# Splitting the transposes around block work, an earlier transpose of first rows, a later reciprocal

## Chip, cores and metric

The kernel runs on one core of a Trainium2 chip. The time is device time in microseconds; the figure compared is the median of several runs. A core has TensorE (PE; its weight loads are listed apart as PEld), VectorE (DVE), ScalarE (ACT), GpSimd (POOL) and SyncE (SP), which run side by side and wait for each other by semaphores.

## What is computed

Top-k attention, then a mixture of experts with one expert per token, all in fp32:

```python
# q, k, v: (B=8, H=8, S=576, D=64)
scores = matmul(q, k.T) / sqrt(D)
kth = partition(scores, -32)[..., -32]            # the 32nd largest of each row
scores = where(scores >= kth, scores, -1e9)
attn = exp(scores - max); attn /= sum(attn) + 1e-9
x = matmul(attn, v)                               # rearranged to (4608 tokens, 512)
logits = x @ w_gate                               # 8 experts
e = argmax(logits); gate = softmax(logits)[e]
y = gate * (relu(x @ w1[e]) @ w2[e])              # w1[e]: 512x1024, w2[e]: 1024x512
```

## The kernel before

The program is a list of 144 *turns*. Each takes two 128-row tiles of scores (128x576 each) through a pipeline that spreads over several turns:

- TensorE multiplies q and k into PSUM (`sc`), three turns ahead; ScalarE copies the result to SBUF (`s`).
- VectorE finds each row's 32nd largest score (`search`: folds into `h`, `l`, `few`, `hl`, then rounds of MAX8 and MATCH_REPLACE8 on `scr`, into `tops`).
- ScalarE (`low`, then `depths`), GpSimd (`less`) and ScalarE again (`weights`, the exponential) make the masked weights `w`.
- One turn later TensorE transposes `w` (`wTm`: 4 transposes for each of the two tiles; `wTl`: the last columns of both) and ScalarE copies the result to `wT` and `wTt`.
- Nine turns make two *units* of two heads. When a unit's tiles are through, `ending` multiplies by v (`po`, twice), turns the result back (`px`) and scales it with the reciprocals `rz` of the rows' sums.
- After 18 turns a batch is complete: its tokens are routed, and rows of one expert form *blocks* of 128 rows. TensorE does the blocks' work in *pieces*, 16 to a block, between the attention's instructions: the rows' transposes (`xtp`, copied to `xTs`), 8 pieces of `ph` (first product), 8 of `py` (second product).

TensorE's, ScalarE's and VectorE's instructions stand in the program as this loop issues them; nothing reorders them later.

```python
def bank(name):                               # two PSUM banks in turn, for all of
    return k.ps_t.tile([P, SM], F32, name=name, tag="t")   # wTm, wTl, po, px, rank

def transposed(tiles, w):
    q = slice(ST + tiles[0][1] * P, ST + (tiles[0][1] + 1) * P)
    for m, (n, i) in enumerate(tiles):
        pm = bank("wTm")
        for c in range(NC):                   # NC = 4
            ...
            nc.tensor.transpose(pm[:, c * P:(c + 1) * P], w[:, m, first:first + P], ident)
        ...                                   # ScalarE empties the bank into wT
    yield
    pt = bank("wTl")
    ...                                       # transposes of the last columns
    yield
    ...                                       # ScalarE copies them to wTt

def block(n, following=..., put_off=...):
    if not hasattr(n, "xT"):
        turned(n)                             # xtp, and the copy to xTs put on `due`
        yield "pause"
    evacuate("xT")
    ...                                       # 8 pieces of ph, 4 products each
    evacuate("h0")
    following()
    yield "pause"
    evacuate()
    ...                                       # 8 pieces of py

def following():
    put_stores()
    if loaded and landed(loaded[0]):
        turned(loaded[0])                     # the next block's rows

def pieces(n):
    nonlocal current, left
    while n > 0 and left > 0:
        if current is None:
            if not landed(loaded[0]):
                break
            current = block(loaded.pop(0), following, stores.append)
            ahead()
        if clock is None:
            evacuate()
        step = next(current)
        if step == "pause":
            if clock is not None:
                break
            continue
        ...

def ending(b, u):                             # yields the place in a turn where it goes on
    ...
    out_steps = outputs(n, x)
    yield "products"
    next(out_steps)                           # po, first half
    yield "relu"
    next(out_steps)                           # ScalarE copies it to oT
    if u % 2 == 0:
        yield "relu"
    div = divisors(n)
    next(div)                                 # ScalarE writes rz
    aside.append(div)                         # VectorE's reciprocal, in the next search
    yield "products"
    next(out_steps)                           # po, second half
    ...
    yield "relu"
    next(out_steps)
    yield "products"
    next(out_steps)                           # px
    yield "relu"
    next(out_steps, None)                     # ScalarE copies it to xl
    yield "rows"
    ...

# the loop over turns, from the scores' copies on
    evacuate()
    at_place("turn")
    turns = turning(i - 1) if i else iter(())
    next(turns, None)                         # wTm, both tiles
    part = min(BETWEEN, now - now // 2)       # BETWEEN = 2
    rest = pieces(part)
    next(turns, None)                         # wTl
    rest = pieces(now - now // 2 - part + rest)
    weights(tiles, w_of[i], nbias)
    next(turns, None)                         # copy to wTt
    evacuate()
    if i + AHEAD + 1 < len(work):
        multiply(i + AHEAD + 1)               # sc
    ...
    at_place("products")                      # po or px, if an ending is at that place
    at_place("weights")
    credit = min(credit + pieces(now // 2 + rest), 6 * rate)
```

Of the kernel before, what the change touches and what calls it, by code (L numbers as in the profile page):

```python
# [35 lines left out]
def kernel(  # L36
# [249 lines left out]
    def fold(s):  # L286

        f = SimpleNamespace()
        f.h = k.att.tile([P, 2, HF], F32, name="h", bufs=1)
        nc.vector.tensor_tensor(f.h, s[:, :, 0, :], s[:, :, 1, :], op=ALU.max)  # L290
        f.l = k.att.tile([P, 2, HF], F32, name="l")
        nc.vector.tensor_tensor(f.l, s[:, :, 0, :], s[:, :, 1, :], op=ALU.min)
        return f
# [8 lines left out]
    aside = []  # L302
# [85 lines left out]
                w[:, m, :], w[:, m, :], AF.Exp, scale=scale, bias=nbias[:, m:m + 1], accum_out=n.z[:, c:c + 1]  # L388
            )

    def transposed(tiles, w):

        q = slice(ST + tiles[0][1] * P, ST + (tiles[0][1] + 1) * P)
        for m, (n, i) in enumerate(tiles):
            pm = bank("wTm")
            for c in range(NC):
                first = c * P + (0 if tails(tiles) else m * ST)
                nc.tensor.transpose(pm[:, c * P:(c + 1) * P], w[:, m, first:first + P], ident)  # L398
            pm4 = pm[:, :].rearrange("p (c q) -> p c q", c=NC)
            if tails(tiles):  # L400
                at = tail_at(n)
                nc.scalar.copy(wT[:, :, :, at:at + ST], pm4.rearrange("p c (h q) -> p c h q", h=2))
            else:
                nc.scalar.copy(wT[:, :, m, q], pm4)  # L404
        yield
        pt = bank("wTl")
        if tails(tiles):
            for a in range(2):
                nc.tensor.transpose(pt[0:ST, a * P:(a + 1) * P], w[:, 1 - a, SM:S], ident)
        else:  # L410
            nc.tensor.transpose(pt[:, 0:P], w[:, :, :].rearrange("p m k -> p (m k)")[:, SM:SM + P], ident)
        yield
        if tails(tiles):
            pt4 = pt[0:ST, 0:2 * P].rearrange("p (a h q) -> p a h q", a=2, h=2)
            for h in range(2):
                both = wTt[h * ST:(h + 1) * ST, :].rearrange("p (a q) -> p a q", q=ST)[:, 0:NT + 1:NT, :]
                nc.scalar.copy(both, pt4[:, :, h, :])
        else:
            nc.scalar.copy(wTt[:, q], pt[:, 0:P])  # L419
# [248 lines left out]
    def evacuate(upto=None):  # L668

        while due and (upto is None or upto in [kind for kind, _ in due]):  # L670
            due.pop(0)[1]()
# [62 lines left out]
    with fast:  # L734
# [9 lines left out]
        waiting, loaded, coming, spare, scatters, stores = [], [], [], [], [], []  # L744
        current = None
        left = clock = 0

        def landed(n):
            return clock is None or clock - n.at >= ON_CHIP
# [16 lines left out]

        def following():
            put_stores()
            if loaded and landed(loaded[0]):
                turned(loaded[0])  # L770

        def pieces(n):
            nonlocal current, left
            while n > 0 and left > 0:
                if current is None:
                    if not landed(loaded[0]):
                        break
                    current = block(loaded.pop(0), following, stores.append)
                    ahead()
# [7 lines that stand above are left out]
                if step == "last":  # L787
                    current = None
                n -= 1
                left -= 1  # L790
            return n
# [11 lines left out]
        def ending(b, u):  # L803

            nonlocal left
            n = unit[b * U + u]
            if u == 0:
                x_of[b] = k.xp.tile([P, KC, XW], F32, name="x")
                in_turn(token_ids(x_of[b][:, :, Dm + 1].bitcast(I32), b))
                lg_of[b] = k.small.tile([P, KC, E], F32, name="lg")  # L810
            x, lg = x_of[b], lg_of[b]
# [6 lines that stand above are left out]
                yield "relu"  # L818
            div = divisors(n)
            next(div)  # L820
            aside.append(div)
            yield "products"
            next(out_steps)
            if b * U + u + 2 < len(units):
                load_values(unit[b * U + u + 2])
            yield "relu"
            next(out_steps)
            yield "products"
            next(out_steps)
            yield "relu"  # L830
            next(out_steps, None)
            yield "rows"
            through(div)
            logits(n, lg)
            rows(n, x)
            if u < U - 1:
                return
            yield "small"
            r = choice(lg)
            aside.append(r.steps)  # L840
            yield "weights"
            yield "turn"
            through(r.steps)
            nc.scalar.activation(lg, lg, AF.Exp)
            yield "products"
            ranks(r)
            yield "small"
            steps = places(r, x)
            aside.append(steps)
            yield "relu"  # L850
            nc.scalar.copy(run, r.run)
            yield "pool"
            through(steps)
            scatters.extend(scattering(r, x))
            if b == B - 1:
                scatter(KC)
                slot_i = k.small.tile([1, 2, NSLOT], I32, name="slot_i")
                through(table(slot_i, SURE, False))
                firsts = [(slot_i[0:1, 0, j:j + 1], slot_i[0:1, 1, j:j + 1]) for j in range(SURE)]
                ready = load_rows(SimpleNamespace(), firsts[0][1], True)  # L860
            new = LAST - SURE if b == B - 1 else new_of[b]
            if new:
                slot_i = slot_last if b == B - 1 else k.small.tile([1, 2, NSLOT], I32, name="slot_i")
                steps = table(slot_i, new, b == B - 1)
                aside.append(steps)
                yield "weights"
                yield "pool"
                yield "weights"
                yield "pool"
                through(steps)  # L870
                coming.extend((slot_i[0:1, 0, j:j + 1], slot_i[0:1, 1, j:j + 1]) for j in range(new))
            if b == B - 1:
                spare.extend(coming[ALWAYS - SURE:])
                del coming[ALWAYS - SURE:]
                assert len(loaded) == 2 and not waiting
                fill_up()
                coming[0:0] = [(firsts[0][0], ready)] + [(expert, (piece,)) for expert, piece in firsts[1:]]
                scatter(0)
# [3 lines left out]
        def at_place(name):  # L882
            for end in list(late):
                if end[1] == name:
                    end[1] = next(end[0], None)
                    if end[1] is None:
                        late.remove(end)
# [3 lines left out]
        def tiles_of(i):  # L891
            b, g = work[i]
            return [(unit[b * U + u], tile) for u, tile in g]

        def turning(i):
            return transposed(tiles_of(i), w_of.pop(i))

        def multiply(i):
            tiles = tiles_of(i)
            got_of[i] = products(tiles)  # L900
            n, tile = tiles[0]
            more = n.b * U + n.u + 2
            if tile == (NC - 1 if n.u % 2 else 2 * NC) and more < len(units):
                unit.append(load_unit(*units[more]))

        def loop():
            nonlocal credit, rate, clock
            for i in range(min(AHEAD, len(work))):
                multiply(i)
                s_of[i], steps = scores(got_of.pop(i))  # L910
                for step in steps:
                    step()
            multiply(AHEAD)
            f_of[0] = fold(s_of[0])
            fold_on(f_of[0])
            for i, (b, g) in enumerate(work):
# [36 lines left out]
                        step()  # L953
                evacuate()
                at_place("turn")
                turns = turning(i - 1) if i else iter(())
                next(turns, None)
                part = min(BETWEEN, now - now // 2)
                rest = pieces(part)
# [1 line left out]
                rest = pieces(now - now // 2 - part + rest)  # L961
                weights(tiles, w_of[i], nbias)
                next(turns, None)
                evacuate()
                if i + AHEAD + 1 < len(work):
                    multiply(i + AHEAD + 1)
                if tile == NC - 1:
                    end = ending(b, u)
                    late.append([end, next(end)])
                at_place("products")  # L970
                at_place("weights")
                credit = min(credit + pieces(now // 2 + rest), 6 * rate)
# [147 lines left out]
```

## Time and profile before

The time before is 1374.14 us, the median of three runs from 1371.75 to 1375.33; the profiled run's span is 1370.3 us.

| engine | busy us | share of the span | instructions |
|---|---|---|---|
| PE | 1234.6 | 90% | 7666 |
| PEld | 838.6 | 61% | 7666 |
| DVE | 1084.5 | 79% | 4591 |
| ACT | 932.0 | 68% | 2113 |
| POOL | 661.5 | 48% | 805 |

The groups that the change touches (mean time of one record; a matmul in fp32 leaves two records or more):

| group | count | busy us | mean ns |
|---|---|---|---|
| PE transposes `wTm` | 1152 | 171.2 | 289 |
| ACT copy `wT` from `wTm`, 128x512 | 256 | 139.1 | 604 |
| PE `ph`, 128x128 | 2560 | 308.6 | 276 |
| PE `py`, 128x512 | 640 | 292.2 | 596 |
| ACT copy `xTs` from `xtp`, 128x512 | 40 | 24.3 | 608 |
| DVE reciprocal `rz`, 128x10 | 32 | 6.4 | 200 |

A line of a wait names the engine that was idle, what it was to do next, and after `<-` what it waited for, with the time. "L398" is line 398 of the kernel. In the timeline a row merges instructions of one kind that follow each other: start, length, engine, line, what is written from what, shapes, how many records, and in brackets the idle time before it.

### The profile page before, as it was taken

What the parts mean: (1) busy time and instruction counts of PE and PEld (TensorE: products, weight loads), DVE (VectorE), ACT (ScalarE), POOL (GpSimd) and SP (SyncE); (2) the same over time, 40 slices, a digit from 0 to 9 for tenths busy, and PEclk for the clock granted to TensorE, in tenths of its full rate; (3) what the DMA queues carried; (4) which work ended last, traced back from release to release, by engine and by line L of the source; (5) the groups of instructions that cost most, each with busy time, mean ns of one, the idle gap of its engine ahead of it and who ended that gap; (6) DMA issues with size and microseconds to landing.
All of it is one profiled execution on the core that took longest, in us unless ns stands there. A gap on an engine that the chain in (4) does not pass through costs nothing. (4 is left out here: it accounts for less than half of the span.)

```text
span 1370.3 us, 24487 instructions
## 1 busy us (share of the span) xinstructions
PE 1234.6 (90%) x7666; PEld 838.6 (61%) x7666; DVE 1084.5 (79%) x4591; ACT 932.0 (68%) x2113; POOL 661.5 (48%) x805
## 2 busy tenths in 40 slices
PE   5777677687799999999999999999999999999995
PEld 3444444344466666766666666767676677776773
DVE  8999999999999999999999999999999820000000
ACT  4788877877888888888877788887777821111110
POOL 3455557555654666566556665565557621000000
PEclk8788787877999999999999999999999999999998
DMA  2100011001583267427654474357542859999880
GB/s 82 29 29 29 28 36 56 29 29 44 178 296 124 89 232 266 142 72 261 226 174 168 166 274 148 113 188 293 184 167 75 308 183 358 390 325 331 301 321 18
DMA packets 102220, 231.68 MB, mean 169 GB/s; under 512 B 5182, under 2 KB 25918, under 8 KB 102080
## 3 DMA queue, kind: packets, MB, share of 16 engines
q1 hardware_dynamic: 95328, 209.76, 43.8%
q0 software_dynamic: 6464, 19.97, 4.0%
q8 instruction: 62, 1.02, 0.3%
q14 instruction: 78, 0.64, 0.1%
q10 hardware_dynamic: 288, 0.30, 0.1%
HBM read 208.72 MB, written 22.33 MB: 169 GB/s over the span
## 5 line engine op out<-in xcount | busy, mean ns | idle before, releaser
L379 POOL TENSOR_TENSOR w<-s,w 128x576 f32<-128x576 f32 x288 | 409.5, 1442 | 432.3 <-ACT w L370 432.3
L687 PE MATMUL ph<-xTs,w 128*128 128x128 f32 x2560 | 308.6, 276 | 6.0 <-ACT xTs L664 6.0
L687 PEld LDWEIGHTS ph<-xTs,w 128*128 128x128 f32 x2560 | 297.4, 192 | 26.4 <-issue 19.1
L702 PE MATMUL py<-w,hT 128*128 128x512 f32 x640 | 292.2, 596 | 0.0
L338 DVE MAX8 tops<-scr 128x8 f32<-128x168 f32 x864 | 245.5, 316 | 0.0
L276 PE MATMUL sc<-qkb 64*128 64x288 f32 (+1 forms) x1280 | 221.6, 472 | 9.5 <-ACT s L283 5.2
L387 ACT ACTIVATE w<-w,nbias 128x576 f32<-128x576 f32 x288 | 224.0, 792 | 3.5 <-POOL w L379 2.5
L370 ACT ACTIVATE w<-s,low 128x576 f32<-128x576 f32 x288 | 207.6, 768 | 4.7
L398 PE MATMUL wTm<-turn,w 128*128 128x128 f32 x1152 | 171.2, 289 | 29.0 <-ACT xl L450 17.7
L398 PEld LDWEIGHTS wTm<-turn,w 128*128 128x128 f32 x1152 | 133.1, 146 | 89.6 <-issue 35.4
L999 DVE CAST any_i<-pd 1x1 int32<-1x1 f32 x1 | 0.1, 146 | 236.0 <-PE pd L997 236.0
L702 PEld LDWEIGHTS py<-w,hT 128*128 128x128 f32 x640 | 114.4, 190 | 117.6 <-issue 116.5
L345 DVE MATCH_REPLACE8 scr<-tops,scr 128x168 f32<-128x168 f32 x576 | 176.9, 311 | 0.0
L283 ACT COPY s<-sc 128x576 f32<-128x576 f32 x288 | 169.1, 641 | 10.5 <-PE sc L276 10.5
L404 ACT COPY wT<-wTm 128x512 f32<-128x512 f32 x256 | 139.1, 604 | 38.9 <-PE wTm L398 38.6
L276 PEld LDWEIGHTS sc<-qkb 64*128 64x128 f32 (+1 forms) x1280 | 118.2, 195 | 72.9 <-issue 26.6
L432 PE MATMUL po<-wT,vb 128*64 128x288 f32 x1024 | 157.8, 457 | 0.4 <-ACT wTt L419 0.4
L708 POOL DMA_INDIRECT out_dram<-y,xg x40 | 43.1, 1078 | 211.9 <-ACT y L716 199.8
L329 DVE MAX8 few<-l 128x8 f32<-128x288 f32 x288 | 127.2, 442 | 0.0
L432 PEld LDWEIGHTS po<-wT,vb 128*64 128x64 f32 x1024 | 75.3, 152 | 78.0 <-issue 29.3
L692 ACT ACTIVATE hT<-ph 128x512 f32<-128x512 f32 x80 | 48.6, 608 | 107.3 <-PE ph L687 107.3
L290 DVE TENSOR_TENSOR h<-s 128x576 f32<-128x576 f32 x144 | 117.0, 812 | 5.8 <-ACT s L283 5.8
(116 smaller groups left out, 1433.4 us busy)
## 6 DMA issues: line engine op xcount, KB each, us to landing
w<-in_moe_w_dram SPq DMA_DIRECT2D x80, 2048.0 KB, 9.6
qkb<-in_qk_dram SPq DMA_DIRECT2D x31, 608.0 KB, 4.3
xg<-x_rows SPq DMA_DIRECT2D x40, 257.0 KB, 10.0
vb<-in_v_dram SPq DMA_DIRECT2D x32, 320.0 KB, 3.2
x_rows<-blank SPq DMA_DIRECT2D x5, 257.0 KB, 14.7
x_rows<-blank POOLq DMA_DIRECT2D x4, 257.0 KB, 8.5
x_rows<-x,posi POOLq DMA_INDIRECT x40, 3.1
out_dram<-y,xg POOLq DMA_INDIRECT x40, 6.1
```

The costliest lines, as they stand in the source:

```text
L276: nc.tensor.matmul(ps[rows, j, 0:HF], n.q[d, cols], n.k[d, keys], start=True, stop=True)
L283: lambda m=m, ps=ps: nc.scalar.copy(s[:, m, :, :], ps[:, :, 0:HF]) for m, ps in enumerate(got)
L338: nc.vector.max(out=tops[:, m, r * 8:(r + 1) * 8], in_=src[m])
L345: nc.vector.match_replace(out=scr[:, m, :], in_to_replace=tops[:, m, r * 8:(r + 1) * 8], in_values=src[m], imm_value=NEG,)
L370: nc.scalar.activation(w[:, m, :], s[:, m, :, :].rearrange("p j k -> p (j k)"), AF.Relu, scale=-STEEP, bias=low[:, m:m + 1],)
L379: k.last_pool = in_turn(nc.gpsimd.tensor_tensor(w[:, m, :], s[:, m, :, :].rearrange("p j k -> p (j k)"), w[:, m, :], op=ALU.subtract)).ins
L387: nc.scalar.activation(w[:, m, :], w[:, m, :], AF.Exp, scale=scale, bias=nbias[:, m:m + 1], accum_out=n.z[:, c:c + 1])
L398: nc.tensor.transpose(pm[:, c * P:(c + 1) * P], w[:, m, first:first + P], ident)
L404: nc.scalar.copy(wT[:, :, m, q], pm4)
L432: nc.tensor.matmul(po[r, 0:HF], n.v[:, c, r], rhs, start=(c == 0), stop=(c == KC - 1))
L687: nc.tensor.matmul(ph[:, f, :], n.w1[:, 0, dt, fc * P:(fc + 1) * P], n.xT[:, dt, :], start=(dt == 0), stop=(dt == DT - 1),)
L702: nc.tensor.matmul(py, hT[:, f, :], n.w2[:, 0, f, :], start=(f == 0), stop=(f == FT - 1))
```

## The change

Three things are done, and no arithmetic is added or removed.

- **Split transposes.** `wTm`, `wTl`, `po`, `px` and `rank` share two PSUM banks in turn. When an ending has put an output into one of them at the end of a turn, the next turn's second `wTm` needs that bank, and ScalarE has to empty it first. After such a turn (`busy_bank`) the second tile's transposes are now issued behind the first two pieces of block work.
- **First blocks' rows ahead.** A block whose predecessor has been finished before its weights had come gets its rows transposed by `block` itself, right ahead of its first product. Now the loop does it ahead of the scores, and `pieces` starts no block whose rows are not transposed.
- **Reciprocal later.** `divisors` joins the queue of side work for VectorE one step of the ending later.

```diff
-    def transposed(tiles, w):
+    def transposed(tiles, w, apart=False):
@@
                 nc.scalar.copy(wT[:, :, m, q], pm4)
-        yield
+            if m == 0 and apart:
+                yield
+        if not apart:
+            yield
         pt = bank("wTl")
@@ def following():
             put_stores()
-            if loaded and landed(loaded[0]):
+            if loaded and landed(loaded[0]) and not hasattr(loaded[0], "xT"):
                 turned(loaded[0])
@@ def pieces(n):
                 if current is None:
-                    if not landed(loaded[0]):
+                    if clock is not None and not hasattr(loaded[0], "xT"):
                         break
                     current = block(loaded.pop(0), following, stores.append)
@@ def ending(b, u):
             div = divisors(n)
             next(div)
-            aside.append(div)
             yield "products"
             next(out_steps)
             if b * U + u + 2 < len(units):
                 load_values(unit[b * U + u + 2])
             yield "relu"
             next(out_steps)
+            aside.append(div)
             yield "products"
@@ the loop
-                turns = turning(i - 1) if i else iter(())
+                turns = turning(i - 1, busy_bank) if i else iter(())
+                busy_bank = False
                 next(turns, None)
                 part = min(BETWEEN, now - now // 2)
                 rest = pieces(part)
@@
                 weights(tiles, w_of[i], nbias)
                 next(turns, None)
+                if current is None:
+                    following()
                 evacuate()
@@
                 if tile == NC - 1:
                     end = ending(b, u)
                     late.append([end, next(end)])
+                busy_bank = any(end[1] == "products" for end in late)
                 at_place("products")
```

(Cut: `turning` passes the flag on, and `busy_bank` starts as False.)

More of the change, by code (lines that the diff above doesn't have):

```diff
@@ L893, in tiles_of, with turning @@
             return [(unit[b * U + u], tile) for u, tile in g]
-        def turning(i):
-            return transposed(tiles_of(i), w_of.pop(i))
+        def turning(i, apart=False):
+            return transposed(tiles_of(i), w_of.pop(i), apart)
         def multiply(i):
@@ L955, in loop @@
                 at_place("turn")
-                turns = turning(i - 1) if i else iter(())
+                turns = turning(i - 1, busy_bank) if i else iter(())
+                busy_bank = False
                 next(turns, None)
```

## The prediction

> **What bounds the kernel now.** I read the page's busy table and its 40 slices first, then the stretches cut where the slices change, then the waits of the middle stretch alone, then the timeline around single waits.
>
> The four stretches (columns: us, then busy time and instruction count of PE, PEld, DVE, ACT and POOL, the granted clock, DMA share, GB/s):
>
> ```profile
> 0.00:350.00 350.00, 253.22 (x1358) 150.64 (x1360) 343.39 (x1482) 270.53 (x624) 182.47 (x246) 0.81 0.12 39
> 350.00:400.00 50.00, 42.53 (x280) 28.89 (x278) 50.00 (x211) 42.72 (x98) 30.45 (x38) 0.97 0.76 273
> 400.00:1090.00 690.00, 675.61 (x4508) 468.72 (x4505) 680.82 (x2847) 568.29 (x1300) 416.14 (x481) 1.00 0.52 184
> 1090.00:1345.00 255.00, 253.24 (x1482) 184.54 (x1481) 9.98 (x51) 48.96 (x93) 31.50 (x40) 1.00 0.85 302
> ```
>
> To 400 us VectorE (the top-32 search) is busy all the time but for the start, and TensorE has time to spare. From 400 to 1090 both are full: TensorE is idle 690 - 675.6 = 14.4 us, VectorE 690 - 680.8 = 9.2 us. From 1090 only expert blocks are left and TensorE alone sets the pace: the scalings of y come every 14.45 us (1326.5, 1340.9). So whatever this change does before 400 us is hidden behind VectorE, the last stretch holds the same blocks in both kernels, and the gain has to come out of the 14.4 us of TensorE and the 9.2 us of VectorE in the middle.
>
> Who waited for whom from 400 to 1090 us (total us, times, longest):
>
> ```profile
> ACT wT L404 <- PE wTm L398: 32.8, 22, 2.0
> ACT oT L434 <- PE po L432: 22.0, 28, 1.6
> ACT wT L402 <- PE wTm L398: 17.9, 9, 4.6
> ...
> PE ph L687 <- ACT xTs L664: 5.3, 5, 1.1
> DVE rz L457 <- ACT rz L455: 4.9, 6, 1.6
> PE wTl L411 <- ACT wT L404: 4.6, 16, 0.5
> DVE h L290 <- ACT s L283: 4.0, 4, 1.1
> ...
> PE wTm L398 <- ACT oT L434: 3.2, 3, 1.1
> ```
>
> With one more line of 1.3 us (the transposes waiting for the copy of xl) TensorE's waits add to 5.3 + 4.6 + 3.2 + 1.3 = 14.4 us, all its idle time. VectorE's two add to 8.9 of its 9.2 us. Two of the waits, on TensorE's timeline:
>
> ```profile
> 476.90 0.66 PE L398 MATMUL wTm<-turn,w 128*128 128x128 f32 x4 [1.11 <-ACT oT L434]
> 477.40 1.06 PE L687 MATMUL ph<-xTs,w 128*128 128x128 f32 x8
> 478.77 0.33 PE L411 MATMUL wTl<-turn,w 128*128 128x128 f32 x1 [0.31 <-ACT wT L404]
> ```
>
> ```profile
> 507.43 1.02 PE L702 MATMUL py<-w,hT 128*128 128x512 f32 x2
> 508.29 0.60 PE L662 MATMUL xtp<-turn,xg 128*128 128x128 f32 x4
> 508.73 0.27 PE L411 MATMUL wTl<-turn,w 128*128 128x128 f32 x1
> 510.06 1.16 PE L687 MATMUL ph<-xTs,w 128*128 128x128 f32 x8 [1.06 <-ACT xTs L664]
> ```
>
> In the first, the second tile's transposes want the bank that still holds an output, and ready block work (ph) stands behind them. In the second, a batch's first block has its rows transposed and its first product wants ScalarE's copy of them at once.
>
> **What the skill says.** The Trainium skill, "PSUM — Partial Sum Buffer", section "Engine vs sequencer instructions", says that TensorE may load weights ahead of matmuls in flight, but that matmuls start and complete in program order. The first timeline agrees: the ready ph products do not pass the waiting transposes (1.11 us). So moving instructions in the program can fill such a wait. The same sentence calls ScalarE's queue strictly first in, first out; that is the danger here, because a copy that must wait for later transposes holds up all of ScalarE. "Perfetto Trace Analysis", "Optimization Strategy", advises to look for gaps on the bounding engine within each regime; the split at 400 us is that. "SBUF — State Buffer", "Who interferes with whom", says that a VectorE instruction with two inputs in SBUF contends with a reading GpSimd instruction. The trace fits: the fold into h, two SBUF inputs, took 0.74 us at 644.29 and 1.68 us at 659.58, where GpSimd's small operations were long too. It adds noise whenever the phase of the engines shifts.
>
> **The change, part by part.** The built programs show what moves. On each engine the number of compute instructions stays. No piece of block work changes its turn except around six first blocks, and the last stretch is untouched.
>
> 1. *Split transposes.* 67 of the 144 turns get "4 transposes, up to two pieces, 4 transposes" for "8 transposes, pieces". None lies before turn 53, which waits near 410 us: earlier there are no pieces. Following TensorE's gaps from turn to turn over 400 to 1090 us, those that lie in a turn that is now split are: 3.2 us (transposes behind oT), 1.3 us (behind xl), and of the 4.6 us of wTl behind the first copy of wT 3.15 us, because two pieces and four transposes now come between. Each such wait, 0.3 to 1.3 us, is shorter than two pieces (1.06 us for ph here, 1.02 us for py, one piece each, so about 2 us). Sum 7.7 us.
> 2. *First blocks' rows ahead.* xtp and its copy move behind the wTl transposes and before the next scores; the first ph follows the scores (8 matmul records 1.24 us at 647.27) instead of standing right behind. The copy of xTs takes 0.63 us, but waits for the two exponentials (0.8 us each and 0.25 us accumulator reads) ahead of it on ScalarE, so perhaps a third of the wait returns in another place. Five waits of 1.06 us: 5.3 us on TensorE, 3.5 to 5.3 us gained.
> 3. *The reciprocal later.* div joins the side queue two turns later, when ScalarE has long written rz. VectorE's 4.9 us in six waits go.
>
> TensorE thus could lose 7.7 + 5 = about 12.5 of its 14.4 us of idle time. But VectorE's 690 us hold only 9.2 us of idle time, and it must do the same searches: it can move forward by 4.9 us for certain, and by the 4.0 us of the wait for s only where TensorE's lead reaches ScalarE. So min(12.5, 8.9) = 8.9 us is the most I can see.
>
> From it I take 2 to 4 us for part 1's price. ScalarE now copies wT's first half and stands until two pieces (1.9 us) and four more transposes (0.66 us) are done, where earlier both halves came together. ScalarE is idle 690 - 568.3 = 121.7 us in the stretch, 1.35 us in each of some 90 turns, so its throughput holds; but where TensorE runs behind, exactly the ACT-behind-PE lines above (32.8 + 17.9 us), the copies of s, and with them VectorE's next fold, come up to 1.9 us later. There the wait for s grows. Net: 5 to 7 us, and I choose 6: 1374.1 - 6 = 1368.
>
> **Rivals.**
> - *TensorE alone sets the pace from 400 us on.* For it: 98% busy, and the tail is pure TensorE. Then all 12.5 us come through: 1361.5. Against it: VectorE is 98.7% busy in the same stretch, and in places ScalarE still waits for VectorE (13.0 us behind tops).
> - *ScalarE becomes the wait.* For it: strict order, 67 turns, up to 1.9 us each, 127 us in all against 121.7 us of idle time. Against it: the delay feeds on itself only if ScalarE is ahead of TensorE; once it is late, the second half is ready when it comes. If a tenth of it reached VectorE the gain would turn into a loss: 1374 - 9 + 13 = 1378.
> - *Everything is hidden.* The lead gained on TensorE is spent waiting for VectorE, and removed rz waits return as waits for s: 1372 to 1374.
>
> **Range and chances.** The sum says 1368; the best rival 1361.5, the worst I take seriously 1378. Before itself ran from 1371.75 to 1375.33, so a median may be off by 2 us. Eight in ten: 1361 to 1376. Two per cent is 27 us, more than all idle time of both engines in the middle stretch, so faster by that gets 0.01; slower by that needs over a quarter of the 127 us of ScalarE delay to reach VectorE: 0.02. Within 2%: 0.97.
>
> **What would show it.** Right: from 400 to 1090 us no line of transposes (wTm) behind oT or xl on PE, no ph behind xTs, no rz on VectorE; PE idle under 5 us there; the wait of the wT copies for wTm on ScalarE well up, from 50.7 us to about 100; the last stretch, from the end of the searches, as long as before. Wrong in part 1 if the waits for s on VectorE rise above 8 us; wrong in part 2 if ph still waits for xTs, or sc for something new; wrong in the choice between the engines if PE's idle time falls by 12 us and the span falls by as much, or if VectorE's searches take longer in sum for contention with GpSimd.

## The result, and the profile after

The changed kernel takes 1387.16 us (median of four runs, 1386.84 to 1387.67) against 1374.21 us before: a ratio of 1.0097, with a 95% interval from 1.008 to 1.0115. It is slower by 13 us; the prediction was 1368 with a range to 1376.

The loss lies in the stretch in which attention and blocks share TensorE. By the trace, turn 52's fold starts at 377.3 us in both kernels, VectorE's last search ends at 1091.0 us before and 1103.7 us after, and from there to the end it takes 279.3 us before and 281.5 us after. So 12.7 us are lost between 377 and 1104 us, and 2.2 us behind it. The granted clock of the middle stretch is 1.00 in both, so the clock is not the reason.

The middle stretch of the kernel after, same columns as in the prediction:

```profile
400.00:1090.00 690.00, 662.48 (x4414) 459.73 (x4411) 677.41 (x2791) 556.84 (x1275) 410.24 (x474) 1.00 0.51 179
```

TensorE's idle time, which the change was to fill, has gone from 14.4 to 27.5 us, VectorE's from 9.2 to 12.6 us. The waits of the kernel after in the same stretch (total us, times, longest):

```profile
ACT wT L404 <- PE wTm L398: 67.3, 62, 1.6
...
ACT wT L402 <- PE wTm L398: 19.7, 14, 3.7
...
PE wTl L414 <- ACT wT L404: 17.3, 29, 1.2
DVE h L290 <- ACT s L283: 11.5, 10, 1.6
...
PE ph L690 <- ACT xTs L667: 6.4, 5, 1.3
...
PE py L705 <- ACT hT L695: 3.6, 5, 1.1
```

Three of the waits that the change aimed at are gone: no transposes (wTm) wait for oT in this stretch, for xl only 0.7 us of their weight loads, and VectorE no longer waits for rz. In their place wTl waits 17.3 us for the copies to wT (4.6 before), py waits for hT, and VectorE's fold waits 11.5 us for s (4.0 before). ph waits for xTs as before (6.4 against 5.3). ScalarE stands 87.0 us waiting for transposes, where it stood 50.7.

One split turn on ScalarE:

```profile
416.58 0.40 ACT L437 COPY oT<-po 128x288 f32<-128x288 f32 x1 [1.23 <-PE po L435]
416.88 1.19 ACT L283 COPY s<-sc 128x576 f32<-128x576 f32 x2
418.10 0.58 ACT L404 COPY wT<-wTm 128x512 f32<-128x512 f32 x1
420.32 0.59 ACT L404 COPY wT<-wTm 128x512 f32<-128x512 f32 x1 [1.64 <-PE wTm L398]
420.80 0.78 ACT L387 ACTIVATE w<-w,nbias 128x576 f32<-128x576 f32 x1
```

and on TensorE:

```profile
417.90 1.95 PE L690 MATMUL ph<-xTs,w 128*128 128x128 f32 x16
419.68 0.60 PE L398 MATMUL wTm<-turn,w 128*128 128x128 f32 x4
```

In the kernel before, the two copies of this turn ran one behind the other:

```profile
417.13 1.07 ACT L404 COPY wT<-wTm 128x512 f32<-128x512 f32 x2
```

Between its two copies ScalarE now stands 1.64 us, while TensorE does the two pieces (1.95 us) that went in between. The exponentials behind start that much later. Here is a turn that is not split, but follows split ones (the first split turn has its transposes at 387.0 us). ScalarE comes late to the first copy:

```profile
403.88 0.69 ACT L719 ACTIVATE y<-py,xg 128x512 f32<-128x512 f32 x1
404.47 1.08 ACT L404 COPY wT<-wTm 128x512 f32<-128x512 f32 x2
```

and TensorE pays:

```profile
405.11 0.33 PE L414 MATMUL wTl<-turn,w 128*128 128x128 f32 x1 [1.09 <-ACT wT L404]
```

wTl needs the bank of the first half, which ScalarE empties only now. In the kernel before, the second copy of this turn had begun by 403.7 us, and wTl did not wait:

```profile
403.68 0.60 ACT L404 COPY wT<-wTm 128x512 f32<-128x512 f32 x1
404.19 0.27 PE L411 MATMUL wTl<-turn,w 128*128 128x128 f32 x1
```

### The profile page after: what moved, and what is told of

The parts are those of the page before. It is cut to its first block, busy times and chain, and to the rows that moved or that the text cites. A ratio compares the mean times of both kernels' runs of the same rounds, so it can differ in the third digit from the quotient of the medians.

```text
span 1385.2 us, 24490 instructions
## 1 busy us (share of the span) xinstructions
PE 1232.3 (89%) x7666; PEld 840.8 (61%) x7666; DVE 1093.9 (79%) x4591; ACT 931.6 (67%) x2113; POOL 663.3 (48%) x805
## 5 line engine op out<-in xcount | busy, mean ns | idle before, releaser
L398 PE MATMUL wTm<-turn,w 128*128 128x128 f32 x1152 | 181.8, 292 | 32.5 <-ACT xl L453 22.0
L398 PEld LDWEIGHTS wTm<-turn,w 128*128 128x128 f32 x1152 | 140.0, 149 | 102.9 <-issue 42.8
L404 ACT COPY wT<-wTm 128x512 f32<-128x512 f32 x256 | 143.9, 598 | 76.9 <-PE wTm L398 76.6
L435 PE MATMUL po<-wT,vb 128*64 128x288 f32 x1024 | 152.6, 445 | 0.4 <-ACT wTt L422 0.4
```

The source lines that it names most:

```text
L435: nc.tensor.matmul(po[r, 0:HF], n.v[:, c, r], rhs, start=(c == 0), stop=(c == KC - 1))
```

## The experiments

The theories, by the letters of the expectations. **A**: ScalarE's standing between the two copies makes it late for all that follows, and TensorE and VectorE wait. **B**: the moved reciprocal is to blame. **C**: the moved rows are. **D**: any interruption of the transposes costs. **E**: it costs that wTl comes right behind the second half. **F**: VectorE's collisions with GpSimd carry the loss. **G** and **H** are about the rows and come below. "Before" was run beside each group and stood at 1373.4 to 1374.35 us; ratios are to it. Idle time is TensorE's from 400 to 1090 us, 690 less its busy time.

### Each part alone

The split alone takes the hunks in `transposed` and in the loop, without the call of `following`.

> The split of the transposes alone, on the kernel before; rows and reciprocal as before. Theory A (ScalarE stands at the second half's copy of wT, comes late to all that follows, and both TensorE and VectorE wait for it): this alone brings nearly all of the loss, 1384 to 1389 us; wTl waits about 15 us for wT on PE, VectorE's tensor-tensor operations collide more with GpSimd. Theory B (moving the reciprocal shifts VectorE's side work against GpSimd): the split alone costs at most 3 us, 1372 to 1377. Theory C (the first rows' move is to blame, because nothing stands between the transposes and wTl in those turns): split alone 1368 to 1374.

Measured: 1390.62 us, ratio 1.0119 [1.0102, 1.0136], TensorE idle 28.3 us. The split alone loses more than the whole change, 17.0 us against the kernel before, and 1.6 us more than A's range allowed.

The rows alone take the hunks in `following` and `pieces` and the call in the loop.

> The first blocks' rows ahead alone. A: 1373 to 1376, because the wait of ph for xTs (6 of about 1.1 us) returns as large as it was. B: the same. C: 1380 or more. The prediction on record counted on 3.5 to 5.3 us less.

Measured: 1375.89 us, ratio 1.0015 [1.0008, 1.0022], idle 14.8 us; ph waits 6.4 us for xTs.

The reciprocal alone takes the hunk in `ending`.

> The later reciprocal alone. A: the 4.9 us of rz waits on VectorE go, 1369 to 1374. B: 1380 or more, with VectorE's busy time up by 5 us or more at an unchanged ScalarE lag. C: as A.

Measured: 1374.33 us, ratio 1.0001 [0.9993, 1.001]. The waits for rz are gone, but VectorE's busy time in the stretch went from 680.8 to 685.3 us, and TensorE's idle time stayed at 14.4 us. B and C named the reciprocal or the rows as the cause of the loss; with the split at 1390.62 us and these two at 1374.33 and 1375.89, both fall.

Both without the split:

> The change without the split: first rows ahead and the later reciprocal. A: 1373 to 1377, the two parts being worth nothing together as they are alone (1375.9 and 1374.3). D: the same.

Measured: 1375.71 us, ratio 1.0012 [1.0003, 1.0021].

### ScalarE's second copy put behind the exponentials

In split turns TensorE's order stays that of the split; only ScalarE's order changes:

```diff
-            ...copy of pm4 to wT, for both tiles as they are transposed
+            if m and apart:
+                later = copied          # the second tile's copy
+            else:
+                copied()
@@ behind the exponentials, ahead of the copy to wTt
+        if apart:
+            later()
```

> The split alone, but in split turns the copy of the second half to wT stands behind the two exponentials on ScalarE instead of ahead of them, so that ScalarE has 2 us of other work while TensorE does the two pieces. A: the loss of the split goes for the most part: 1368 to 1376, ScalarE's wait for wTm falls from near 70 us to under 45. B and C: no different from the split alone.

Measured: 1372.02 us, ratio 0.999 [0.9981, 0.9999], idle 15.1 us: 18.6 us less than the split alone (1390.62), by the order of one copy on ScalarE. The same split turn as above, on ScalarE:

```profile
417.81 0.58 ACT L406 COPY wT<-wTm 128x512 f32<-128x512 f32 x1
418.29 0.78 ACT L387 ACTIVATE w<-w,nbias 128x576 f32<-128x576 f32 x1
...
420.03 0.59 ACT L406 COPY wT<-wTm 128x512 f32<-128x512 f32 x1
```

The two exponentials fill the time of the two pieces. The waits of this kernel in the stretch:

```profile
ACT wT L406 <- PE wTm L398: 32.0, 22, 2.0
...
ACT wT L404 <- PE wTm L398: 17.7, 9, 4.5
...
PE wTl L421 <- ACT wT L406: 8.4, 16, 1.2
```

The two lines together are 49.7 us, against 90.9 with the split alone and 50.7 before. (The expectation's "near 70 us to under 45" fits the larger line alone, 71.2 us with the split alone and 32.0 here.) wTl keeps 8.4 us against 4.6 before, which uses up most of what the split saves elsewhere. A is right about the cause: TensorE's order is the same in the two kernels, and the loss is gone.

What the split then brings is told by the counterpart, TensorE's order of before with the later copy in the same turns:

> The kernel before with TensorE's order untouched; only ScalarE's copy of the second half goes behind the exponentials in the same 67 turns. It tells what the split itself brings in the repaired version (1372.0 with it, 1373.7 before). A: 1372 to 1376, since the halves come together there; if it is at or below 1372 the split brings nothing.

Measured: 1372.45 us, ratio 0.9988 [0.9981, 0.9995]. That is the repaired split's time within both intervals: no gain of the split itself is seen.

### One piece instead of two

```diff
-                part = min(BETWEEN, now - now // 2)
+                part = min(1 if busy_bank else BETWEEN, now - now // 2)
```

(Cut: the line also moves up, ahead of `busy_bank = False`.)

> The split alone, but with at most one piece between the halves instead of two; the other piece goes behind wTl. Theory A (the loss is the time that ScalarE stands between the two copies): about half the loss of the split alone, 1379 to 1384, against 1374 before and 1391 with two pieces; ScalarE's wait for wTm between those two. Rival D (any interruption of the transposes costs, for the extra waits of wTl behind wT): as the split alone, 1388 to 1392.

Measured: 1388.86 us, ratio 1.0105 [1.0088, 1.0122], idle 24.8 us. Not half. A as worded missed, D had it. But this edit also moves the other piece behind wTl, so that TensorE reaches wTl one piece earlier after the first half. The next run keeps that distance: first half, piece, second half, piece, wTl.

> The split alone, with one piece between the halves and the other piece between the second half and wTl, so that as much TensorE work stands between the first half and wTl as before (the first try with one piece, 1388.9, took that away). A (ScalarE's standing between the two copies): 1378 to 1385, about half of the 17 us. D (any interruption costs): 1387 to 1392. E (what costs is that wTl comes right behind the second half): back to 1373 to 1377.

Measured: 1377.55 us, ratio 1.0026 [1.0017, 1.0035], idle 17.2 us. D falls. The time lies between E's range and A's, half a microsecond from each. E by itself can't be the cause: in the kernel with the later copy wTl also comes right behind the second half, and there is no loss. TensorE's wait for the copies, with one piece and wTl right behind the second half:

```profile
PE wTl L414 <- ACT wT L404: 16.8, 43, 1.2
```

and with the second piece ahead of wTl:

```profile
PE wTl L413 <- ACT wT L404: 9.1, 18, 1.2
```

So there are two ways to the same wait. wTl waits when ScalarE is late with the first half's copy, and when TensorE comes to it too soon. With wTl at the same distance from the first half, one piece between the halves costs 3 us and two cost 17. That is out of proportion, but wTl's place behind the second half differs between the two as well, so it is not shown that the standing alone is so steep. ScalarE's spare time, 1.35 us a turn on average by the prediction, would cover a piece (0.95 us) but not two; that was not measured apart.

### GpSimd's subtraction left out

Here the step `less` is left out and the exponential takes s, so the attention is not masked and other tokens go to other experts, while the number of blocks stays (2560 records of `ph` in all). The two times are read first of all as a pair.

```diff
-        nc.gpsimd.tensor_tensor(w[:, m, :], s[...], w[:, m, :], op=ALU.subtract)
-        nc.scalar.activation(w[:, m, :], w[:, m, :], AF.Exp, ...)
+        nc.scalar.activation(w[:, m, :], s[...], AF.Exp, ...)
```

> The kernel before with GpSimd's subtraction (less) left out: the exponential takes s itself, so the attention is not masked. GpSimd's large reads are gone from the stretch. No theory says much of this time by itself; if VectorE's collisions with GpSimd held the kernel back it is 10 us or more below 1374, if TensorE sets the pace it stays above 1366. It is the base for the next run.

> The same without the subtraction, with the split. A (ScalarE late, TensorE waits for it): 10 us or more above the run without the subtraction and without the split, as with the subtraction (17 us). Rival F (the loss is VectorE's: ScalarE's shift moves GpSimd's subtraction onto VectorE's two-input operations, whose busy time rose 5 to 10 us): at most 5 us above.

Measured: 1364.43 us (ratio 0.9932 [0.991, 0.9953]) without the split and 1384.39 us (1.0083 [1.0056, 1.0111]) with it. The middle stretch without the split:

```profile
400.00:1090.00 690.00, 678.82 (x4520) 470.81 (x4519) 657.22 (x2837) 569.39 (x1305) 218.90 (x306) 1.00 0.54 186
```

and with it:

```profile
400.00:1090.00 690.00, 663.90 (x4440) 461.90 (x4438) 650.57 (x2791) 558.78 (x1279) 207.93 (x298) 1.00 0.53 183
```

The split costs 20 us here too, although VectorE had 32.8 us to spare, so F falls. The first line shows more: VectorE's busy time in the stretch is down 23.6 us (680.8 to 657.2), yet the kernel is only 9.9 us faster, short of both limits that I had set. Some of that is won earlier: by the traces turn 52's fold starts at 374.7 us instead of 377.3, and from there to the end of the searches it takes 709.8 us instead of 713.7. So about 4 us came out of the middle, where TensorE's 14.4 us of idle time have shrunk to 11.2. I read this as TensorE, with its waits for ScalarE, setting most of the pace there.

### The whole change repaired, and the rows

The whole change with the later copy, and the split with the later copy and the later reciprocal, without the rows:

> The whole change, with the one repair: in split turns the second half's copy stands behind the exponentials. A: 1368 to 1373, at or below the split with that repair alone (1372.0). D: 1380 or more.

> The split with the repaired copy and the later reciprocal; first rows as before. A: 1367 to 1373; if VectorE's own waits bound the stretch, the 5.3 us of waits for rz come through and it is 5 us below 1372.0, if TensorE sets the pace it is the same.

Measured: 1375.8 us (1.0016 [1.0009, 1.0023]) and 1370.49 us (0.9976 [0.9965, 0.9987]). The first missed A's range by 3 us; the difference between the two is the rows' part, which costs 5 us here. Why it costs at all, one timeline tells, of the rows alone on TensorE:

```profile
509.53 0.60 PE L662 MATMUL xtp<-turn,xg 128*128 128x128 f32 x4
510.06 1.24 PE L276 MATMUL sc<-qkb 64*128 64x288 f32 x8
512.59 2.61 PE L687 MATMUL ph<-xTs,w 128*128 128x128 f32 x21 [1.29 <-ACT xTs L664]
```

and on ScalarE:

```profile
509.65 0.82 ACT L387 ACTIVATE w<-w,nbias 128x576 f32<-128x576 f32 x1
...
511.90 0.63 ACT L664 COPY xTs<-xtp 128x512 f32<-128x512 f32 x1
```

The rows are transposed at 510.1 us and copied from 511.9 us, for two exponentials, a copy (wTt) and a scaling of y stand in between. In the kernel before, the copy stood ahead of the exponentials:

```profile
509.38 0.63 ACT L664 COPY xTs<-xtp 128x512 f32<-128x512 f32 x1
```

**G** says that this order is why the part brings nothing, **H** that TensorE waits for ScalarE in any case. The edit:

```diff
+                if current is None:
+                    following()
+                    evacuate()
                 weights(tiles, w_of[i], nbias)
                 next(turns, None)
-                if current is None:
-                    following()
                 evacuate()
```

> The first rows ahead alone, but with ScalarE's copy to xTs ahead of the two exponentials instead of behind them. If the exponentials are why part 2 brought nothing (theory G), ph no longer waits for xTs (under 1 us in all, against 5.3 before and 6.4 with the part as made) and the time falls by up to 5 us, 1369 to 1373. If the wait only moves on (theory H: TensorE then waits elsewhere for the same ScalarE), 1373 to 1377 with ph's wait gone.

Measured: 1368.27 us, ratio 0.9965 [0.9952, 0.9979], below what G expected. On ScalarE the copy starts 1.7 us earlier, ahead of the exponentials:

```profile
510.19 0.64 ACT L664 COPY xTs<-xtp 128x512 f32<-128x512 f32 x1
510.65 0.83 ACT L387 ACTIVATE w<-w,nbias 128x576 f32<-128x576 f32 x1
```

and the middle stretch is

```profile
400.00:1090.00 690.00, 679.99 (x4522) 470.39 (x4521) 680.44 (x2853) 571.47 (x1310) 417.48 (x488) 1.00 0.52 186
```

TensorE's idle time is 10.0 us, 4.4 less than before, no product (ph) waits for xTs any more, and the kernel is 5.1 us faster. G is right.

Two attempts to get below that. wTl behind all the pieces ahead of the scores, on top of the repaired split with the later reciprocal:

> The repaired split with the later reciprocal (1370.5), and wTl behind all the pieces that precede the scores. The 8.7 us that wTl waits for wT there should shrink to 3 or less. If TensorE's idle time is what sets the pace, 1365 to 1369; if something else holds, 1370 or more.

Measured: 1371.17 us, ratio 0.9983 [0.9977, 0.999]. wTl still waits 6.4 us for wT, far above the expectation, and VectorE is busy 689.0 of 690 us. Then everything with both repairs:

> The whole change with both repairs (second copy and xTs copy placed on ScalarE as in the runs before). G: below the repaired split with the later reciprocal (1370.5), 1366 to 1370. H: 1370 to 1374.

Measured: 1371.56 us, ratio 0.9985 [0.9978, 0.9992]: no better than the repaired split with the reciprocal, and 3.3 us slower than the repaired rows alone. That is H's range, though H's reason was refuted above. Why these parts do not add is not settled. With wTl behind the pieces VectorE has nothing left to give, but with everything it is still idle 6.8 us. There no `ph` waits for xTs, but wTl waits 9.1 us for wT (4.6 before), and TensorE's idle time is 14.2 us, as before: what the parts saved has come back in other waits for ScalarE.

## Why the prediction was wrong

**The bound.** The prediction took the smaller of two idle times and made VectorE the limit. Taking 23.6 us of busy time from VectorE gained 9.9, and only about 4 of these in the middle stretch; taking 5.3 us of waits for xTs from TensorE gained 5.1, of which 4.4 by the traces in that stretch (709.3 us instead of 713.7). So the rival "TensorE alone sets the pace" was nearer. It does not hold alone: with wTl behind the pieces VectorE is busy 689.0 of 690 us while TensorE still has 14.0 us idle, and no kernel here that does the whole work has a median under 1368 us. This choice does not explain the sign of the result, since by either engine the prediction's sum was a gain.

**Part 1: part of the benefit came, the price was far too low.** The waits behind oT and xl went (3.2 and 1.3 us). The step that failed is "From it I take 2 to 4 us for part 1's price", with its reason, that ScalarE's idle time of 1.35 us a turn keeps its throughput. The wait of ScalarE for wTm rose by 36.3 us, less than the 50 I expected. But not all of it vanished in ScalarE's idle time: with the whole change wTl waits 12.7 us more for wT and py 3.6 us for hT on TensorE, and VectorE waits 7.5 us more for s. I had looked for it only at the last of these. That ScalarE's standing is behind the loss is shown by the later copy, which takes 18.6 us off with TensorE's order unchanged. The step that wTl would lose 3.15 us failed the same way: the distance to the first half was kept, but the copy came later. The split alone measured 17 us of loss where the prediction had a gain. The rival "ScalarE becomes the wait" named the mechanism. Its size, a tenth of 127 us, looks near to 17 us only by luck: ScalarE's wait rose by 36.3 us, not 127, and a loss about half as large came of it, with the gain of 9 us that the rival set against it not there. The reading that split turns begin near 410 us was off too, by no great matter: the first has its transposes at 387.0 us.

**Part 2.** The estimate of 3.5 to 5.3 us gained assumed that a third of the wait returns. All of it returned, 6.4 us for 5.3, because the copy to xTs went behind the exponentials. The prediction named that queue and undersized it. With the copy ahead of them the part is worth 5.1 us, so its mechanism was right.

**Part 3.** "VectorE's 4.9 us go" was right, and the time did not fall (1.0001). Two reasons are possible and not told apart: TensorE set the pace, or the search lost what the waits had freed, for its two-input operations took 3.6 us longer (248.0 us against 244.4).

**What held.** The stretch before 377 us is unchanged. The last stretch is nearly so: 281.5 us, where the traces of the kernels that lose 3 us or less have 279.1 to 281.8. The whole change loses 4 us less than the split alone, though its other parts alone lose 0 and 2 us; why is open too.

## What to carry to other kernels

When work is put between two halves of something, look at the engine that empties the halves: if its queue is strictly in order, it stands for as long as the work that was put in, unless its own ready work is put there too. Move a producer and its consumer's place in the other engine's program together. Idle time averaged over a stretch (1.35 us a turn here) does not tell that a wait of 1.6 us in a turn is free; look at the next instruction that needs that engine.

## What was not expected of the hardware

- Removing waits of VectorE made its own work longer: with the reciprocal moved alone, the two-input operations of the search (the folds into h, l, few and hl, as many as before) took 248.0 us against 244.4, from turn 52 on. Without GpSimd's subtraction, and without the split, they took 229.7 us, so some 15 us of their time before seem to hang on that subtraction running beside them.
- One piece more between the halves, about 1 us of TensorE work in a turn, made 13 us of difference in the whole (1377.6 with one, 1390.6 with two, wTl at the same distance from the first half), where the first piece cost 3. How much of this is ScalarE's standing and how much wTl's place behind the second half is open.
